# Seven instead of eight tiles transposed by TensorE in a 2:4 sparse projection, with one PSUM bank used in halves

## The chip, the cores and the metric

The kernel runs on one core of one Trainium2 chip. The metric is the device time of one execution in microseconds (us), less being better. A run's time is compared as the median of several executions; the profile is of one execution of its own.

## The reference

A weight matrix is pruned to a 2:4 pattern along its rows: in each group of four neighbouring rows, per column, the two entries that are largest in magnitude stay (ties with the second largest stay too). Then a batch of tokens is multiplied by it and a bias is added.

```python
B, S, D = 16, 512, 1024        # x: (B, S, D), w: (D, D), b: (D), all bfloat16
N, M = 2, 4
wg = w.reshape(G, M, D)
mag = jnp.abs(wg)
order = jnp.argsort(mag, 1)
thr = jnp.take_along_axis(mag, order[:, M - N:M - N + 1, :], 1)
wp = (wg * (mag >= thr)).reshape(D, D)
return jnp.einsum("bsd,df->bsf", x, wp) + b
```

## The kernel before

The 8192 tokens are 64 tiles of 128. One tile needs 16 matmuls of 128 x 128 weights against 512 columns: eight pieces of the contraction, two halves of the output columns (h = 0 and 1). TensorE needs each tile of x transposed, as its stationary operand. This is done in two ways, and the tiles are split accordingly.

**The front: the first T = 8 tiles.** While the weights are still being loaded and pruned, TensorE transposes the first eight tiles itself, in two halves g of the contraction (512 rows of the weights each). `transpose_half(g, t, bk)` (line 148) issues four transposes of 128 x 128 into the PSUM bank `bk` (line 152) and a copy on ScalarE that takes the result to the tile `xT` (line 154). In the front the contraction is split by the row within the group of four (m = 0 to 3), so that VectorE can compare the four rows without moving them between partitions.

The weights are pruned in `pieces` (line 51), each a half g and a range of columns: 0 to 128, 128 to 256 and 256 to 512 of g = 0, then 0 to 256 and 256 to 512 of g = 1 (these five are output half 0), then 512 to 1024 of g = 0 and of g = 1. `abs_piece` (line 109) takes the magnitudes, on VectorE or, for the pieces in `ABS_ON_ACT`, on ScalarE; `prep_piece` (line 120) is seven instructions on VectorE that end with the pruned piece of `wp`. `mm_piece(i, t)` (line 157) multiplies tile t by piece i: four matmuls (line 161) into the columns of bank t that belong to the piece.

There are eight PSUM banks. Tile t accumulates in bank t. The transposes of g = 0 of tile t go through bank t, ahead of its accumulation. Those of g = 1 go in turn through banks 6 and 7, and so tiles 6 and 7 begin to accumulate only after the last of these have been copied out.

The order of the front is written out by hand in the string `FRONT` (line 208), token by token; each engine gets its instructions in this order. `W` is a warm-up matmul on zeros into bank 7, `A` and `P` are the magnitudes and the pruning of a piece, `Tgt` a transpose of half g of tile t, `Mit` piece i times tile t, `Vt` the copy of output half 0 of tile t from its bank to a staging tile on ScalarE (line 176), `St` the bias added to that on VectorE (line 180), `Ugh` four DMAs that move pruned weights to the natural order of rows, tile `wp_nat` (line 144), and `Bn` the issue of the transposed load of the n-th batch of tiles (line 197). After the string a loop multiplies each of the tiles by the last piece, adds the bias (`evac_dve`, line 184) and stores the tile (line 188).

**The rest: natural tiles.** The other tiles are loaded transposed by DMA, in `batches` (line 202): tiles 8 to 11, then six batches of eight, then the last four. They use `wp_nat` and accumulate all eight pieces of the contraction in banks that are taken in turn by `next_bank`. Batch 0 does all its tiles for h = 0 and then for h = 1 (line 249); the others do both halves of a tile together (line 287). The last tile is done in four quarters.

SyncE's queue issues most loads of x and weights (lines 69 and 76), the bias, the transposed loads and the unpacks, in this order; ScalarE's queue issues a part of the first loads and the stores. There are ten output tiles `o_sb`.

Of the kernel before, what the change touches and what calls it, by code (L numbers as in the profile page):

```python
# [10 lines left out]
def kernel(  # L11
# [8 lines left out]
    P = 128  # L20
    bf16 = mybir.dt.bfloat16
# [6 lines left out]
    B, S, D = x.shape  # L28
    Dout = w.shape[1]
    KT = D // P  # L30
    NTOK = B * S
    NT = NTOK // P
    FH = 512
    KH = D // 2
    assert D == 1024 and Dout == 1024 and NT >= 24
    xf = x.flatten_outer_dims()
    of = out.flatten_outer_dims()

    T = 8

    const = ctx.enter_context(tc.tile_pool(name="const", bufs=1))
    tmp = ctx.enter_context(tc.tile_pool(name="tmp", bufs=2))
# [4 lines left out]
    bank = [psum.tile([P, FH], fp32, name=f"bank{i}") for i in range(8)]  # L47
# [1 line left out]

    wv = w.rearrange("(g p m) f -> p g m f", g=2, m=4)  # L50
    pieces = [(0, 0, 128), (0, 128, 256), (0, 256, 512), (1, 0, 256), (1, 256, 512),
              (0, 512, 1024), (1, 512, 1024)]
    loads = {"A": (0, 0, 256), "B": (0, 256, 512), "C": (1, 0, 512), "D": (0, 512, 1024), "E": (1, 512, 1024)}
    w_ld = {k: const.tile([P, 4, c1 - c0], bf16, name=f"w_{k}") for k, (g, c0, c1) in loads.items()}
    wp_gh = {(g, h): const.tile([P, 4, FH], bf16, name=f"wp_{g}_{h}") for g in range(2) for h in range(2)}
# [7 lines left out]
    def wp_of(i):  # L63
        g, c0, c1 = pieces[i]
        return wp_gh[(g, c0 // FH)][:, :, c0 % FH:c0 % FH + c1 - c0]

    def load_w(k, eng=nc.sync, m0=0, m1=4):
        g, c0, c1 = loads[k]
        K(eng.dma_start(w_ld[k][:, m0:m1, :], wv[:, g, m0:m1, c0:c1]))  # L69
# [3 lines left out]
    def load_x(g, ta, tb, eng=nc.sync):  # L73
        xt = const.tile([P, tb - ta, KH], bf16, name=f"xh_{g}_{ta}")
        src = xf[ta * P:tb * P, g * KH:(g + 1) * KH].rearrange("(t p) c -> p t c", p=P)
        K(eng.dma_start(xt[:], src))
        for t in range(ta, tb):
            xh[(g, t)] = xt[:, t - ta, :]
# [4 lines left out]
    load_x(0, 2, 4, nc.scalar)  # L83
    load_w("B")
    load_x(0, 4, 6, nc.scalar)
    load_x(0, 6, 8)
    load_x(1, 0, 2)
    load_w("C")
    load_x(1, 2, 4)
    load_x(1, 4, 8)  # L90
    load_w("D")
    load_w("E")
    bias_sb = const.tile([P, Dout], bf16, name="bias_sb")
# [9 lines left out]
    def warm(n):  # L103
        for _ in range(n):
            K(nc.tensor.matmul(bank[7][:], lhsT=zeros[:, :P], rhs=zeros[:], start=True, stop=True))  # L105
# [3 lines left out]
    def abs_piece(i, on_act):  # L109
        g, c0, c1 = pieces[i]  # L110
        n = c1 - c0
        mag = const.tile([P, 4, n], bf16, name=f"mag_{i}")[:]
        if on_act:
            K(nc.scalar.activation(mag, w_of(i), Act.Abs))
        else:
            K(nc.vector.tensor_single_scalar(
                mag.bitcast(u16), w_of(i).bitcast(u16), 0x7FFF, op=Alu.bitwise_and))
        mags[i] = mag

    def prep_piece(i):  # L120
        g, c0, c1 = pieces[i]
        n = c1 - c0
        mag = mags.pop(i)
        magv = mag.rearrange("p (a j) f -> p a j f", j=2)
        hi = tmp.tile([P, 2, FH], bf16, name="hi")[:, :, :n]
        lo = tmp.tile([P, 2, FH], bf16, name="lo")[:, :, :n]
        K(nc.vector.tensor_tensor(hi, magv[:, :, 0, :], magv[:, :, 1, :], op=Alu.max))  # L127
        K(nc.vector.tensor_tensor(lo, magv[:, :, 0, :], magv[:, :, 1, :], op=Alu.min))  # L128
        t1 = tmp.tile([P, FH], bf16, name="t1")[:, :n]
        t2 = tmp.tile([P, FH], bf16, name="t2")[:, :n]  # L130
        K(nc.vector.tensor_tensor(t1, hi[:, 0, :], hi[:, 1, :], op=Alu.min))  # L131
        K(nc.vector.tensor_tensor(t2, lo[:, 0, :], lo[:, 1, :], op=Alu.max))
        thr = tmp.tile([P, FH], bf16, name="thr")[:, :n]
        K(nc.vector.tensor_tensor(thr, t1, t2, op=Alu.max))  # L134
        mask = tmp.tile([P, 4, FH], bf16, name="mask")[:, :, :n]
        K(nc.vector.tensor_tensor(mask, mag, thr[:, None, :].to_broadcast([P, 4, n]), op=Alu.is_ge))  # L136
        K(nc.vector.tensor_tensor(wp_of(i), w_of(i), mask, op=Alu.mult))
# [4 lines left out]
    def unpack(g, h):  # L142
        for j in range(4):
            K(nc.sync.dma_start(wp_nat[h][:, 4 * g + j, :], wp_gh[(g, h)][32 * j:32 * (j + 1), :, :]))

    xT = {}

    def transpose_half(g, t, bk):
        xv = xh[(g, t)].rearrange("p (q m) -> p m q", m=4)
        dst = bank[bk][:].bitcast(bf16)[:, :4 * P].rearrange("p (m q) -> p m q", m=4)  # L150
        for m in range(4):
            K(nc.tensor.transpose(dst[:, m, :], xv[:, m, :], ident[:]))  # L152
        xt = const.tile([P, 4, P], bf16, name=f"xT_{g}_{t}")
        K(nc.scalar.copy(xt[:], dst))  # L154
        xT[(g, t)] = xt

    def mm_piece(i, t, start=False, stop=False):
        g, c0, c1 = pieces[i]
        o = c0 % FH
        for m in range(4):  # L160
            K(nc.tensor.matmul(  # L161
                bank[t][:, o:o + c1 - c0], lhsT=xT[(g, t)][:, m, :], rhs=wp_of(i)[:, m, :],
                start=start and m == 0, stop=stop and m == 3))
# [10 lines left out]
    def evac_act(t):  # L174
        st = const.tile([P, FH], fp32, name=f"stage{t}")
        K(nc.scalar.copy(st[:], bank[t][:]))  # L176
        stage[t] = st

    def add_staged(t, h):
        K(nc.vector.tensor_tensor(  # L180
            get_o(t)[:, h * FH:(h + 1) * FH], stage.pop(t)[:], bias_sb[:, h * FH:(h + 1) * FH], op=Alu.add))

    def evac_dve(t, h, bk):
        K(nc.vector.tensor_tensor(  # L184
            get_o(t)[:, h * FH:(h + 1) * FH], bank[bk][:], bias_sb[:, h * FH:(h + 1) * FH], op=Alu.add))

    def store(t):
        K(nc.scalar.dma_start(of[t * P:(t + 1) * P, :], out_tiles.pop(t)[:]))
# [3 lines left out]
    def issue_batch(t0, nb):  # L192
        if nb < 8:
            xt = const.tile([P, KT, nb * P], bf16, name=f"xTs{t0}")
        else:
            xt = xtb.tile([P, KT, nb * P], bf16, name="xTb")
        K(nc.sync.dma_start_transpose(out=xt[:], in_=xf[t0 * P:(t0 + nb) * P, :]))
        for j in range(nb):
            xN[t0 + j] = xt[:, :, j * P:(j + 1) * P]


    batches = [(8, 4)] + [(t, 8) for t in range(12, NT - 4, 8)] + [(NT - 4, 4)]

    FRONT = """
        W W W W W W W A0 A1 T00 T01 W T02 T03 P0 M00 M01 T04 T05 M02 M03 T06 T07 P1 M04 M10 M11 M05 M12 A2 T10
        M13 T11 M14 M15 T12 P2 T13 A3 M20 T14 T15 M21 M22 T16 A5 M23 T17 P3 M24 M25 A4 M30 M31 M06 M32 A6 M07  # L210
        M16 M17 M26 P4 M27 M33 M34 M35 M36 M37 M40 V0 M41 V1 M42 V2 M43 V3 M44 V4 M45 V5 M46 V6 M47 V7
        P5 B0 U00 U10 U01 M50 M51 M52 M53 M54 M55 M56 M57 P6 U11 B1 B2
        S0 S1 S2 S3 S4 S5 S6 S7
    """
    ABS_ON_ACT = (1, 5, 6)
    for tok in FRONT.split():
        k, n = tok[0], [int(c) for c in tok[1:]]
        if k == "W":
            warm(1)
        elif k == "A":  # L220
            abs_piece(n[0], n[0] in ABS_ON_ACT)
        elif k == "P":
            prep_piece(n[0])
        elif k == "T":
            g, t = n
            transpose_half(g, t, t if g == 0 else 6 + t % 2)
        elif k == "M":
            i, t = n
            mm_piece(i, t, start=i in (0, 5), stop=i in (4, 6))
        elif k == "V":  # L230
            evac_act(n[0])
        elif k == "S":
            add_staged(n[0], 0)
        elif k == "U":
            unpack(*n)
        elif k == "B":
            issue_batch(*batches[n[0]])

    for t in range(T):
        mm_piece(6, t, stop=True)  # L240
        evac_dve(t, 1, t)
        store(t)


    nbk = [0]

    def mm_nat(t, h, bk, c0=0, c1=FH):
        for kt in range(KT):
# [3 lines left out]
    def next_bank():  # L252
        bk = nbk[0] % 8
        nbk[0] += 1
        return bk
# [12 lines left out]
    for bi, (t0, nb) in enumerate(batches):  # L268
        if bi >= 1 and bi + 2 < len(batches):
            issue_batch(*batches[bi + 2])  # L270
        if bi == 0:
            for h in range(2):
                for t in range(t0, t0 + nb):
                    bk = next_bank()
# [5 lines left out]
        for t in range(t0, t0 + nb):  # L280
# [4 lines left out]
            for kt in range(KT):  # L285
                for h in range(2):
                    K(nc.tensor.matmul(bank[bks[h]][:], lhsT=xN[t][:, kt, :], rhs=wp_nat[h][:, kt, :],  # L287
                                       start=kt == 0, stop=kt == KT - 1))
# [33 lines left out]
```

## Time and profile before

| | |
|---|---|
| median of 3 runs | 237.2 us (237.07 to 237.66) |
| profiled execution | 236.98 us, of which the span of the instructions is 235.2 |
| TensorE matmuls busy | 228.7 us, 97% of the span |
| TensorE weight loads busy | 113.4 us, 48% |
| VectorE busy | 106.3 us, 45% |
| ScalarE busy | 18.1 us, 8% |
| line 287, natural tiles | 800 matmuls recorded, 175.6 us busy |
| line 161, front matmuls | 222 recorded, 29.3 us busy |
| line 249, batch 0 and the last tile | 95 recorded, 17.6 us busy |
| line 152, transposes | 64, 5.8 us busy |
| line 154, copies of transposed tiles | 16, 8.5 us busy, 591 ns each |
| HBM read and written | 4.46 MB and 16.78 MB, 90 GB/s over the span |

Engines are PE (TensorE), PEld (its weight loads, which overlap with its matmuls), DVE (VectorE), ACT (ScalarE), POOL and SP (SyncE); a q behind the name is the engine's instruction queue, here where it issues DMAs. Matmuls are pipelined: one lasts longer than the distance to the next one's start, so that distance is what it costs in a stream. Times inside the span count from its start. Some matmul records are missing in the trace.

### The profile page before, as it was taken

Reading aid. Unit: us, or ns where it says so; the run is one execution under the profiler, and the core shown is the slowest. Engines: PE = TensorE matmul, PEld = TensorE weight load, DVE = VectorE, ACT = ScalarE, POOL = GpSimd, SP = SyncE. Lnnn points to the kernel's source line nnn. Section 1 sums busy time; section 2 is a strip of 40 time slices with the busy share of each in tenths; the row PEclk is TensorE's granted clock in tenths of the full one; section 3 lists DMA queues with packets and bytes.
Section 4 is the critical chain, followed back from the end, with each engine's and each line's share of the span. In section 5 each row is a group of like instructions: output and inputs, shape, how many; then the busy total and the mean of one; then the engine's idle time right before and its main releaser. Section 6 shows DMA issues by size and latency. Waiting matters only on the chain.

```text
span 235.2 us, 2901 instructions
## 1 busy us (share of the span) xinstructions
PE 228.7 (97%) x1189; PEld 113.4 (48%) x1208; DVE 106.3 (45%) x184; ACT 18.1 (8%) x29; POOL 0.7 (0%) x6
## 2 busy tenths in 40 slices
PE   7999999999999999999999999999999999999994
PEld 3889544444444444444444444444444444444453
DVE  4999986342432442343343244234334424423433
ACT  4885400000000000000000000000000000000000
POOL 1000000000000000000000000000000000000000
PEclk9999999999999999999999999999999999999999
DMA  6999799999622299215972289421999221122122
GB/s 203 331 256 242 172 232 273 289 199 222 224 89 92 69 259 251 76 61 147 233 201 92 89 175 251 153 85 56 225 282 245 96 89 63 70 89 91 46 89 89
DMA packets 74524, 38.19 MB, mean 162 GB/s; under 512 B 59152, under 2 KB 66320, under 8 KB 74512
## 3 DMA queue, kind: packets, MB, share of 16 engines
q1 hardware_dynamic: 64624, 20.84, 42.9%
q10 hardware_dynamic: 9888, 17.17, 21.0%
q8 instruction: 9, 0.15, 0.2%
q14 instruction: 3, 0.02, 0.0%
HBM read 4.46 MB, written 16.78 MB: 90 GB/s over the span
## 4 chain that ended last, share of the span: by engine, by line
PE 93%; DMA 4%; issue 1%; ACT 0%; SPq 0%; DVE 0%
PE bank L287 75%; PE bank L161 11%; PE bank L249 7%; DMA xh<-in_x_dram 3%; DMA w_A<-in_w_dram 1%; PE bank L152 1%; ACT xT L154 0%; SPq L69 0%; DVE o_sb L265 0%
## 5 line engine op out<-in xcount | busy, mean ns | idle before, releaser
L287 PE MATMUL bank<-wp_nat,xTb 128*128 128x512 bf16 x753 | 165.1, 379 | 0.8
L184 DVE TENSOR_TENSOR o_sb<-bank,bias_sb 128x512 bf16<-128x512 f32 x118 | 76.7, 686 | 120.9 <-PE bank L287 108.7
L287 PEld LDWEIGHTS <-xTb 128*128 128x128 bf16 x768 | 75.1, 98 | 90.6
L161 PE MATMUL bank<-wp,xT 128*128 128x256 bf16 (+2 forms) x222 | 29.3, 287 | 0.1
L161 PEld LDWEIGHTS <-xT 128*128 128x128 bf16 x224 | 19.3, 98 | 8.4
L249 PE MATMUL bank<-wp_nat,xTs 128*128 128x512 bf16 (+1 forms) x95 | 17.6, 343 | 0.1
L249 PEld LDWEIGHTS <-xTs 128*128 128x128 bf16 x96 | 9.4, 98 | 8.2
L287 PE MATMUL bank<-wp_nat,xTs 128*128 128x512 bf16 x47 | 10.5, 379 | 0.1
L154 ACT COPY xT<-bank 128x512 bf16<-128x512 bf16 x16 | 8.5, 591 | 3.0 <-PE bank L152 2.9
L287 PEld LDWEIGHTS <-xTs 128*128 128x128 bf16 x48 | 4.7, 98 | 5.7
L152 PE MATMUL bank<-ident,xh 128*128 128x128 bf16 x64 | 5.8, 232 | 1.3 <-DMA xh<-in_x_dram 0.9
L152 PEld LDWEIGHTS <-xh 128*128 128x128 bf16 x64 | 4.5, 119 | 3.2 <-DMA xh<-in_x_dram 2.8
L136 DVE TENSOR_TENSOR mask<-mag,thr 128x1024 bf16<-128x1024 bf16 (+2 forms) x7 | 5.4, 769 | 0.2
L180 DVE TENSOR_TENSOR o_sb<-stage,bias_sb 128x512 bf16<-128x512 f32 x8 | 4.9, 682 | 0.0
L105 PE MATMUL bank<-zeros 128*128 128x512 bf16 x8 | 3.7, 613 | 1.2 <-DVE zeros L97 1.2
L176 ACT COPY stage<-bank 128x512 f32<-128x512 f32 x8 | 4.0, 623 | 2.6 <-PE bank L161 2.6
L127 DVE TENSOR_TENSOR hi<-mag 128x512 bf16<-128x512 bf16 (+2 forms) x7 | 3.2, 460 | 0.1
L128 DVE TENSOR_TENSOR lo<-mag 128x512 bf16<-128x512 bf16 (+2 forms) x7 | 3.2, 455 | 0.0
L134 DVE TENSOR_TENSOR thr<-t,t 128x256 bf16<-128x256 bf16 (+2 forms) x7 | 2.2, 311 | 0.2
L105 PEld LDWEIGHTS <-zeros 128*128 128x128 bf16 x8 | 1.0, 140 | 2.6 <-issue 1.4
L265 DVE TENSOR_TENSOR o_sb<-bank,bias_sb 128x256 bf16<-128x256 f32 x4 | 1.7, 422 | 1.2 <-PE bank L249 1.2
L131 DVE TENSOR_TENSOR t<-hi 128x256 bf16<-128x256 bf16 (+2 forms) x7 | 2.1, 303 | 0.0
(21 smaller groups left out, 16.2 us busy)
## 6 DMA issues: line engine op xcount, KB each, us to landing
out_dram<-o_sb ACTq DMA_DIRECT2D x63, 256.0 KB, 2.1
wp_nat<-wp SPq DMA_DIRECT2D x16, 128.0 KB, 2.8
xh<-in_x_dram SPq DMA_DIRECT2D x4, 256.0 KB, 5.7
xh<-in_x_dram ACTq DMA_DIRECT2D x2, 256.0 KB, 4.8
w_C<-in_w_dram SPq DMA_DIRECT2D x1, 512.0 KB, 6.9
xh<-in_x_dram SPq DMA_DIRECT2D x1, 512.0 KB, 7.2
w_D<-in_w_dram SPq DMA_DIRECT2D x1, 512.0 KB, 8.3
w_E<-in_w_dram SPq DMA_DIRECT2D x1, 512.0 KB, 9.9
```

Source lines behind the costliest of these rows:

```text
L105: K(nc.tensor.matmul(bank[7][:], lhsT=zeros[:, :P], rhs=zeros[:], start=True, stop=True))
L127: K(nc.vector.tensor_tensor(hi, magv[:, :, 0, :], magv[:, :, 1, :], op=Alu.max))
L128: K(nc.vector.tensor_tensor(lo, magv[:, :, 0, :], magv[:, :, 1, :], op=Alu.min))
L136: K(nc.vector.tensor_tensor(mask, mag, thr[:, None, :].to_broadcast([P, 4, n]), op=Alu.is_ge))
L152: K(nc.tensor.transpose(dst[:, m, :], xv[:, m, :], ident[:]))
L154: K(nc.scalar.copy(xt[:], dst))
L161: K(nc.tensor.matmul(bank[t][:, o:o + c1 - c0], lhsT=xT[(g, t)][:, m, :], rhs=wp_of(i)[:, m, :], start=start and m == 0, stop=stop and m = ...
L176: K(nc.scalar.copy(st[:], bank[t][:]))
L180: K(nc.vector.tensor_tensor(get_o(t)[:, h * FH:(h + 1) * FH], stage.pop(t)[:], bias_sb[:, h * FH:(h + 1) * FH], op=Alu.add))
L184: K(nc.vector.tensor_tensor(get_o(t)[:, h * FH:(h + 1) * FH], bank[bk][:], bias_sb[:, h * FH:(h + 1) * FH], op=Alu.add))
L249: K(nc.tensor.matmul(bank[bk][:, :c1 - c0], lhsT=xN[t][:, kt, :], rhs=wp_nat[h][:, kt, c0:c1], start=kt == 0, stop=kt == KT - 1))
L287: K(nc.tensor.matmul(bank[bks[h]][:], lhsT=xN[t][:, kt, :], rhs=wp_nat[h][:, kt, :], start=kt == 0, stop=kt == KT - 1))
```

## The change

Seven tiles are transposed by TensorE, T = 7, and tile 7 joins batch 0 of the natural tiles, which has five tiles then; natural tiles take bank 7 first. Bank 7 has no accumulating tile any more. The second-half transposes go through it alone, into its first 1024 bytes per partition for even tiles and its second 1024 bytes for odd ones. Output half 1 is pruned and multiplied in four pieces of 256 columns instead of two of 512, the magnitudes of all four on ScalarE. The hand-written order is new: all eight warm-up matmuls come first, T04 and T05 stand ahead of M01, the two transposes T10 and T11 follow each other, as do T12 and T13, and the magnitudes of the last pieces follow the last transpose.

```diff
-    T = 8
+    T = 7
...
     pieces = [(0, 0, 128), (0, 128, 256), (0, 256, 512), (1, 0, 256), (1, 256, 512),
-              (0, 512, 1024), (1, 512, 1024)]
+              (0, 512, 768), (0, 768, 1024), (1, 512, 768), (1, 768, 1024)]
...
-    load_x(0, 6, 8)
+    load_x(0, 6, 7)
...
-    load_x(1, 4, 8)
+    load_x(1, 4, 7)
...
-    def transpose_half(g, t, bk):
+    def transpose_half(g, t, bk, slot):
         xv = xh[(g, t)].rearrange("p (q m) -> p m q", m=4)
-        dst = bank[bk][:].bitcast(bf16)[:, :4 * P].rearrange("p (m q) -> p m q", m=4)
+        dst = bank[bk][:].bitcast(bf16)[:, slot * 4 * P:(slot + 1) * 4 * P].rearrange("p (m q) -> p m q", m=4)
...
-    batches = [(8, 4)] + [(t, 8) for t in range(12, NT - 4, 8)] + [(NT - 4, 4)]
+    batches = [(T, 12 - T)] + [(t, 8) for t in range(12, NT - 4, 8)] + [(NT - 4, 4)]
...
     FRONT = """
-        W W W W W W W A0 A1 T00 T01 W T02 T03 P0 M00 M01 T04 T05 M02 M03 T06 T07 P1 M04 M10 M11 M05 M12 A2 T10
-        M13 T11 M14 M15 T12 P2 T13 A3 M20 T14 T15 M21 M22 T16 A5 M23 T17 P3 M24 M25 A4 M30 M31 M06 M32 A6 M07
-        M16 M17 M26 P4 M27 M33 M34 M35 M36 M37 M40 V0 M41 V1 M42 V2 M43 V3 M44 V4 M45 V5 M46 V6 M47 V7
-        P5 B0 U00 U10 U01 M50 M51 M52 M53 M54 M55 M56 M57 P6 U11 B1 B2
-        S0 S1 S2 S3 S4 S5 S6 S7
+        W W W W W W W W A0 A1 T00 T01 T02 T03 P0 M00 T04 T05 M01 M02 M03 P1 A2 T06 M10 M04 M11 T10 T11 M05 M06
+        M12 M13 M14 M15 M16 P2 A3 M20 M21 T12 T13 M22 T14 M23 T15 M24 P3 T16 A5 A4 M25 M26 M30 A6 M31 M32 A7
+        M33 M34 P4 A8 M35 M36 M40 M41 V0 M42 V1 M43 V2 P5 B0 U00 U10 M44 V3 M45 V4 M46 V5 M50 V6 M51 M52 M53 P6
+        U01 M54 M55 M56 M60 M61 M62 P7 M63 M64 M65 M66 M70 M71 M72 P8 U11 B1 B2 M73 M74 M75 M76
+        S0 S1 S2 S3 S4 S5 S6
     """
-    ABS_ON_ACT = (1, 5, 6)
+    ABS_ON_ACT = (1, 5, 6, 7, 8)
...
-            transpose_half(g, t, t if g == 0 else 6 + t % 2)
+            transpose_half(g, t, t if g == 0 else 7, 0 if g == 0 else t % 2)
...
-            mm_piece(i, t, start=i in (0, 5), stop=i in (4, 6))
+            mm_piece(i, t, start=i in (0, 5), stop=i in (4, 8))
...
     for t in range(T):
-        mm_piece(6, t, stop=True)
+        mm_piece(8, t, stop=True)
...
-    nbk = [0]
+    nbk = [T]
```

More of the change, by code (lines that the diff above doesn't have):

```diff
@@ L34 @@
     KH = D // 2
-    assert D == 1024 and Dout == 1024 and NT >= 24
+    assert D == 1024 and Dout == 1024 and NT >= 24 and NT % 8 == 0
     xf = x.flatten_outer_dims()
     of = out.flatten_outer_dims()
-    T = 8
+    T = 7
     const = ctx.enter_context(tc.tile_pool(name="const", bufs=1))
```

## The prediction

> **What bounds the kernel now.** I read the engines first, then the timeline of the opening, then the table by stage and single DMA issues. Columns of a timeline row: start in us, length in us, engine, line, instruction, count, and in brackets the idle time before it with what ended it.
>
> ```profile
> PE 228.7 (97%) x1189; PEld 113.4 (48%) x1208; DVE 106.3 (45%) x184; ACT 18.1 (8%) x29; POOL 0.7 (0%) x6
> ```
>
> TensorE is the bound; nothing else is above half. So the time is what TensorE does plus what it waits.
>
> ```profile
> 4.86:15.11 10.25, 9.43 (x129) 8.37 (x130) 9.77 (x29) 7.80 (x15) 0.00 (x0) 1.00 1.05 336
> 15.11:38.60 23.49, 23.39 (x161) 14.97 (x162) 21.62 (x36) 8.24 (x12) 0.00 (x0) 1.00 1.02 211
> 38.60:52.42 13.82, 13.77 (x65) 6.25 (x64) 5.57 (x9) 0.00 (x0) 0.00 (x0) 1.00 1.21 259
> ```
>
> In the table by stage (stretch, length, then busy time and count of PE, PEld, DVE, ACT, POOL, clock, DMA) the only real idle time of PE lies before 15.11. From 38.60, the first matmul of line 249, everything streams: 64 matmuls of 512 columns in 13.82 us, 0.2158 us each. Whatever the change does is settled between the first transpose at 4.86 and that first natural matmul.
>
> ```profile
> 8.14 0.64 PE L152 MATMUL bank<-ident,xh 128*128 128x128 bf16 x8
> ...
> 9.73 0.39 PE L152 MATMUL bank<-ident,xh 128*128 128x128 bf16 x4
> ...
> 9.95 0.39 PE L161 MATMUL bank<-wp,xT 128*128 128x128 bf16 x4
> ...
> 10.15 1.07 ACT L154 COPY xT<-bank 128x512 bf16<-128x512 bf16 x2 [0.49 <-PE bank L152]
> 10.17 0.39 PE L152 MATMUL bank<-ident,xh 128*128 128x128 bf16 x4
> ...
> 11.36 0.64 PE L152 MATMUL bank<-ident,xh 128*128 128x128 bf16 x8 [0.35 <-DMA xh<-in_x_dram]
> ...
> 12.88 0.64 PE L152 MATMUL bank<-ident,xh 128*128 128x128 bf16 x8 [0.45 <-ACT xT L154]
> ...
> 13.36 1.04 PE L161 MATMUL bank<-wp,xT 128*128 128x256 bf16 x8
> ...
> 14.23 0.39 PE L152 MATMUL bank<-ident,xh 128*128 128x128 bf16 x4
> ...
> 14.45 0.60 PE L161 MATMUL bank<-wp,xT 128*128 128x256 bf16 x4
> 14.65 0.59 ACT L154 COPY xT<-bank 128x512 bf16<-128x512 bf16 x1 [0.24 <-PE bank L152]
> ```
>
> A matmul's cost is the distance to the next start. Transpose or 128 columns: 9.73 to 9.95 is four, 0.056 us each. 256 columns: 13.36 to 14.23 is eight, 0.109 us each. A token T or a 128-column M is thus 0.224, a 256-column M 0.437, a 512-column M 0.863. T10 goes into bank 6 and T11 (10.17) into bank 7 while ScalarE copies bank 6 out (10.15): two banks, no wait. The waits before 15.11 are those at 11.36 (T12, 0.52, its x) and 12.88 (T14, 0.61, its x), plus 0.11 and 0.19 before T04 (7.03) and T06 (8.14).
>
> One handover matters below. Transposes start at 14.23, their copy at 14.65: 0.42 later (0.45 when PE had been waiting, 12.88 to 13.33). The copy lasts 0.59. And from a copy's end to a waiting matmul:
>
> ```profile
> 16.95 0.58 ACT L154 COPY xT<-bank 128x512 bf16<-128x512 bf16 x1
> ...
> 17.57 0.33 PE L161 MATMUL bank<-wp,xT 128*128 128x128 bf16 x3
> ```
>
> M07 needs this copy, T17's, out of bank 7. It ends at 17.53; 0.05 later PE starts. So from the start of transposes to the start of something that needs their bank back: 0.42 + 0.59 + 0.05 = 1.06 us (1.09 after a wait).
>
> **The change, part by part.** *Tile 7 leaves the front.* T07 and T17, eight transposes, go: -0.45. Its 28 front matmuls cost 8 x 0.056 + 12 x 0.109 + 8 x 0.216 = 3.48; as a natural tile it costs 16 x 0.2158 = 3.45: -0.03. *Last pieces of 256:* 56 matmuls of 512 become 112 of 256: 56 x (0.2184 - 0.2158) = +0.15. *The eighth W:* it leaves its place between T01 and T02 for the idle 0.50 us ahead of 4.86, where its 0.43 fits; M00 can start at 6.25 instead of 6.47: -0.22.
>
> *Bank 7 in halves.* In the changed program as built, the first transposes of T11, T12, ... T16 each wait for a count of ScalarE that the copy of the tile **directly before** raises: T11 for the copy of T10, not T12 for the copy of T10. The halves differ in address only; the wait is on the bank. So two slots work as one, and each of these transposes waits out the 1.06 us less what stands between. T10/T11 and T12/T13 are adjacent in the list: 1.06 - 0.22 = 0.84 each. Ahead of T14, T15 and T16 one 256-column M stands: 1.09 - 0.25 - 0.44 = 0.40 each. Together 2.88 us. No row of before shows PE writing a bank while another engine reads it. The Trainium skill (PSUM — Partial Sum Buffer, section on bank collisions) says that two engines must not touch the same bank in the same partitions at once, whatever the address, and advises to guard by bank. By that rule halves of a bank can't serve as two buffers, and the 2.88 stands; by addresses alone it would be nothing.
>
> *Order of the front.* T04 T05 now stand ahead of M01. Their x lands no sooner:
>
> ```profile
> L76 ACTq DMA_DIRECT2D xh<-in_x_dram x1: 493/493/493, 1.8 to 1.8; - x1
> ...
> DMA to landing us min/median/max: 5.2/5.2/5.2
> ```
>
> Issued at 1.8, landed at 7.0, and T04 can't start before 7.03, as now. M00 ends at 6.47, so PE idles 0.56, which eats the W's gain and more. The other x loads lose 128 KB twice; 512 KB took 1.5 us here (landings behind the waits at 11.36 and 12.88), so the x of T06 and T10 lands 0.37 earlier and that of T14 0.75 earlier: none of them is waited for any more.
>
> The walk: T04 at 7.03; T05, M01, M02, M03 to 8.15; T06, M10, M04, M11 to 9.04; T10 at 9.04, T11 at 10.10; M05 M06 and M12 to M16 to 11.92; M20 (its piece, P2, is done at 11.08) and M21 to 12.80; T12, then T13 at 13.86; M22; T14 at 14.95; M23; T15 at 16.04; M24; T16 at 17.13, ending 17.38. From there 44 M's of 256 columns are left (M25, M26 and seven each of pieces 3 to 8): 44 x 0.437 = 19.23, to **36.61**. Five natural tiles take 5 x 16 x 0.2158 = 17.27, to 53.88, where batch 1 now starts at 52.42: **+1.46 us**. The same by terms: -0.45 - 0.03 + 0.15 - 0.22, waits gone 0.11 + 0.19 + 0.52 + 0.61 + 0.06 = -1.49, waits new 0.56 + 2.88 = +3.44, restarts after waits +0.06: +1.46. From batch 1 on nothing differs.
>
> **What must stay hidden.** *VectorE.* A 256-column piece with its abs on ScalarE takes 2.94 (14.77 to the end of its product at 17.71). ScalarE starts the abs of piece 5 only after T16's copy, at 18.1 instead of 15.13, ready near 19.15 (1.05, between 0.62 for 512 elements and 1.91 for 2048); VectorE idles 1.4 us there. P5 to P8 end at 22.1, 25.0, 28.0, 30.9; M50, M60, M70, M80 ask at 24.4, 27.4, 30.5, 33.5. Cover 2.3 us or more each. Then S0 to S6 (0.60 each) end at 35.2 and the seven evacuations at 39.4, late by 2.8; the natural tiles take bank 7 first and bank 0 at 38.3, evacuated at 35.9. *SyncE's queue.* The transposed load of four tiles was issued in 8.97 and landed in 11.0; eight took 15.5. Five land by 26 at worst, needed at 36.6; its issue takes 8.97 x 5/4, to 21.5, and the eight unpacks of half 0 behind it 0.7 each (sixteen went from 19.36 to 30.63), to 27.1. U11 waits for P8 (30.9), so B1 goes at 33.7 instead of 30.67 and lands at 49.2, needed at 53.9; B2 moves as much and has far more room. *Output tiles:* 12 for 10 buffers as before; tiles 10 and 11 wait for the first two stores, which ends one VectorE wait near 46, when that bank is not needed before 57.
>
> The profiled execution took 236.98, so it would take 238.4; the runs' median is 237.2, 0.22 above it: **238.7 us**.
>
> **Rivals.** *The halves do overlap* (the change does what it says): T12 then waits for T10's copy only. The 2.88 goes, 0.18 before T14 and 0.06 before M20 (P2) come: front ends at 33.87, -1.27, so 235.9: faster. Against it: the waits stand in the program. It decides only if T11 starts while T10's copy runs. 0.05. *The stalls stay but are cheaper:* T04's x lands half a microsecond earlier, or copies hand over faster; -0.6 to -0.9 leaves 237.7, inside 0.3% (0.7 us, about what a measurement here tells from no change). 0.09. *VectorE becomes the bound:* if half-size pieces cost as much as whole ones (4.85, from 17.63 to 22.48), P8 ends at 38.6 and the front at 41.7: +6.5, 243.7. It decides from 3.6 us a piece; the 2.94 of pieces 3 and 4 speaks against it. 0.03. *The transposed loads come late:* batch 1 waits if B1 lands after 53.9, that is 20.2 us after its issue; the longest of before took 17.8. Say one us late: 239.7. 0.03.
>
> **How the numbers follow.** The forecast has 0.80. Its own unknowns: T04's wait 0 to 0.6, each of five handovers within 0.1, the runs' scatter of 0.6 around the median: 238.0 to 239.4. Faster 0.05, same 0.10, slower 0.85.
>
> **What would show it.** Five waits of PE's line 152 for ScalarE's line 154, two near 0.84 and three near 0.40; no wait for x after 7.03; the first natural matmul at 36.6 and batch 1 at 53.9. Copies of one half running beside transposes of the other would prove it wrong, as would PE waiting for a piece or for the transposed x.

## The result and the profile after

| | before | changed |
|---|---|---|
| median | 237.07 us (237.01 to 237.66, 5 runs) | 238.82 us (238.30 to 239.75, 5 runs) |
| ratio, 95% interval | | 1.007 (1.0044 to 1.0096) |
| profiled execution, its span | 236.98, 235.2 | 238.60, 236.8 |
| first natural matmul (line 249) | 38.60 | 36.78 |
| first matmul of batch 1 (line 287) | 52.42 | 54.05 |

The change makes the kernel 1.75 us slower. The profiled executions differ by 1.62 us and batch 1 starts 1.63 us later, so the whole difference has arisen by then. The front is 1.82 us shorter, but one natural tile more costs 3.45.

The table by stage of the changed kernel (stretch, length, then busy time and count of PE, PEld, DVE, ACT, POOL, clock, DMA share, GB/s):

```profile
4.68:17.56 12.88, 10.14 (x133) 9.11 (x133) 12.26 (x35) 7.22 (x13) 0.00 (x0) 1.00 1.09 299
17.56:36.78 19.22, 19.22 (x181) 17.22 (x178) 17.31 (x40) 7.89 (x12) 0.00 (x0) 1.00 0.77 176
36.78:54.05 17.27, 17.16 (x81) 7.84 (x81) 8.50 (x14) 0.00 (x0) 0.00 (x0) 1.00 1.21 251
54.05:234.20 180.15, 178.93 (x833) 82.85 (x847) 67.92 (x107) 0.00 (x0) 0.00 (x0) 1.00 0.52 142
```

From 17.56 on PE waits for nothing (busy shares under 100% there come from matmul records that the trace lacks). Before that it idles 2.74 us out of 12.88. What it waits for stands in the list of waits (engine and line, what was waited for: us in all, times, longest):

```profile
PE bank L152 <- ACT xT L154: 2.1, 5, 0.7
PEld L152 <- DMA xh<-in_x_dram: 1.7, 2, 0.9
...
PE bank L152 <- DMA xh<-in_x_dram: 0.7, 1, 0.7
```

Five times a transpose waits for a copy of the line 154; the list for before has one such entry of 0.4, at 12.88, where the weight load names T14's x instead, which landed then. The timeline of the changed kernel shows each of the five, from T04 to the last transpose:

```profile
7.36 0.64 PE L152 MATMUL bank<-ident,xh 128*128 128x128 bf16 x8 [0.68 <-DMA xh<-in_x_dram]
...
9.40 0.39 PE L152 MATMUL bank<-ident,xh 128*128 128x128 bf16 x4
...
9.82 0.59 ACT L154 COPY xT<-bank 128x512 bf16<-128x512 bf16 x1 [0.31 <-PE bank L152]
10.46 0.38 PE L152 MATMUL bank<-ident,xh 128*128 128x128 bf16 x4 [0.68 <-ACT xT L154]
...
13.11 0.39 PE L152 MATMUL bank<-ident,xh 128*128 128x128 bf16 x4
13.54 0.58 ACT L154 COPY xT<-bank 128x512 bf16<-128x512 bf16 x1 [2.08 <-PE bank L152]
...
14.17 0.38 PE L152 MATMUL bank<-ident,xh 128*128 128x128 bf16 x4 [0.67 <-ACT xT L154]
...
15.23 0.38 PE L152 MATMUL bank<-ident,xh 128*128 128x128 bf16 x4 [0.24 <-ACT xT L154]
...
16.29 0.38 PE L152 MATMUL bank<-ident,xh 128*128 128x128 bf16 x4 [0.24 <-ACT xT L154]
...
17.34 0.38 PE L152 MATMUL bank<-ident,xh 128*128 128x128 bf16 x4 [0.24 <-ACT xT L154]
```

T10 goes at 9.40, its copy at 9.82, and T11, into the other half of the bank, at 10.46, right behind the copy. The same from T12 (13.11) to T13 (14.17) to T14 (15.23), and on to T15 (16.29) and T16 (17.34): always 1.05 to 1.06 us from transposes to transposes, whichever half they use. The idle time in brackets is counted from the modelled end of the matmul before, which lies 0.16 behind the point at which PE could have issued the next (9.40 + 0.39 against 9.40 + 4 x 0.056). With it, 0.68 and 0.24 become the 0.84 that an adjacent pair loses and the 0.40 of the others. Two and three of them are 2.88 us.

T04 waits at 7.36 for its x. That load was issued at 1.8 in both profiles and landed 5.2 us later before, 5.5 here:

```profile
L76 ACTq DMA_DIRECT2D xh<-in_x_dram x1: 491/491/491, 1.8 to 1.8; - x1
...
DMA to landing us min/median/max: 5.5/5.5/5.5
```

### The profile page after: what moved, and what is told of

Read it like the earlier page. It is cut to its first block, busy times and chain, and to the rows that moved or that the text cites. A ratio compares the mean times of both kernels' runs of the same rounds, so it can differ in the third digit from the quotient of the medians.

```text
span 236.8 us, 2986 instructions
## 1 busy us (share of the span) xinstructions
PE 228.9 (97%) x1226; PEld 118.1 (50%) x1244; DVE 107.3 (45%) x198; ACT 17.1 (7%) x28; POOL 0.7 (0%) x6
## 4 chain that ended last, share of the span: by engine, by line
PE 94%; DMA 2%; ACT 1%; issue 1%; ACTq 0%; DVE 0%
PE bank L287 74%; PE bank L161 10%; PE bank L249 9%; DMA xh<-in_x_dram 2%; PE bank L152 1%; ACT xT L154 1%; ACTq L76 0%; ACTq L69 0%; DVE o_sb L265 0%
## 5 line engine op out<-in xcount | busy, mean ns | idle before, releaser
L161 PE MATMUL bank<-wp,xT 128*128 128x256 bf16 (+1 forms) x252 | 25.8, 261 | 0.0
L161 PEld LDWEIGHTS <-xT 128*128 128x128 bf16 x252 | 22.2, 98 | 2.1
L249 PE MATMUL bank<-wp_nat,xTs 128*128 128x512 bf16 (+1 forms) x110 | 21.0, 348 | 0.1
L249 PEld LDWEIGHTS <-xTs 128*128 128x128 bf16 x112 | 11.0, 98 | 9.8
L287 PEld LDWEIGHTS <-xTs 128*128 128x128 bf16 x48 | 4.7, 97 | 5.7
L136 DVE TENSOR_TENSOR mask<-mag,thr 128x1024 bf16<-128x1024 bf16 (+1 forms) x9 | 5.7, 633 | 0.3
L127 DVE TENSOR_TENSOR hi<-mag 128x512 bf16<-128x512 bf16 (+1 forms) x9 | 3.5, 392 | 1.6 <-ACT mag L114 1.5
L128 DVE TENSOR_TENSOR lo<-mag 128x512 bf16<-128x512 bf16 (+1 forms) x9 | 3.5, 389 | 0.0
L134 DVE TENSOR_TENSOR thr<-t,t 128x256 bf16<-128x256 bf16 (+1 forms) x9 | 2.5, 277 | 0.3
L131 DVE TENSOR_TENSOR t<-hi 128x256 bf16<-128x256 bf16 (+1 forms) x9 | 2.4, 269 | 0.0
L132 DVE TENSOR_TENSOR t<-lo 128x256 bf16<-128x256 bf16 (+1 forms) x9 | 2.4, 269 | 0.0
```

The lines of the kernel that those rows point to most:

```text
L161: K(nc.tensor.matmul(bank[t][:, o:o + c1 - c0], lhsT=xT[(g, t)][:, m, :], rhs=wp_of(i)[:, m, :], start=start and m == 0, stop=stop and m = ...
L249: K(nc.tensor.matmul(bank[bk][:, :c1 - c0], lhsT=xN[t][:, kt, :], rhs=wp_nat[h][:, kt, c0:c1], start=kt == 0, stop=kt == KT - 1))
```

## Experiments

Two figures are read from each profile: the start of the first natural matmul, which is the front's end, and its distance from the start of T04. The second leaves out how late T04's x happened to land, and everything else that stands ahead of T04; between the two nothing in the changed kernel waits for a load. In the changed kernel it is 36.78 - 7.36 = 29.42 us; the table takes it from unrounded times. The kernel before ran beside each group (medians 237.07 to 237.15, and 236.96 beside the last two runs).

| run | median us (range) | ratio to before, 95% interval | T04 | front's end | distance |
|---|---|---|---|---|---|
| change | 238.82 (238.30 to 239.75) | 1.0070 (1.0044 to 1.0096) | 7.36 | 36.78 | 29.42 |
| one half only | 238.38 (238.29 to 238.66) | 1.0054 (1.0040 to 1.0067) | 7.20 | 36.61 | 29.41 |
| spread out | 235.97 (235.57 to 236.28) | 0.9951 (0.9937 to 0.9965) | 7.21 | 33.77 | 26.56 |
| two banks | 236.28 (236.15 to 236.36) | 0.9962 (0.9950 to 0.9975) | 6.80 | 34.34 | 27.53 |
| pieces of 512 | 238.75 (238.68 to 239.34) | 1.0073 (1.0061 to 1.0086) | 6.99 | 36.92 | 29.93 |
| one pair back | 236.53 (236.17 to 237.54) | 0.9971 (0.9956 to 0.9986) | 7.11 | 34.67 | 27.56 |
| W back | 239.24 (238.98 to 240.13) | 1.0097 (1.0073 to 1.0121) | 7.74 | 37.16 | 29.42 |
| M01 first | 238.26 (238.19 to 238.52) | 1.0045 (1.0029 to 1.0062) | 7.29 | 36.46 | 29.17 |
| filled | 235.66 (235.41 to 236.11) | 0.9935 (0.9921 to 0.9950) | 7.43 | 33.58 | 26.15 |
| change again | 238.59 (238.27 to 240.34) | 1.0077 (1.0052 to 1.0102) | 7.58 | 37.00 | 29.42 |
| W back again | 238.67 (238.06 to 240.25) | 1.0075 (1.0049 to 1.0102) | 7.89 | 37.30 | 29.42 |

### Only one half of the bank

```diff
-            transpose_half(g, t, t if g == 0 else 7, 0 if g == 0 else t % 2)
+            transpose_half(g, t, t if g == 0 else 7, 0)
```

> All second-half transposes of the changed kernel go into the first half of bank 7; the order and all else stay. Theory (the wait is on the bank, so the second half adds nothing): the first matmul of line 249 stays at 36.8 us, the five waits for the copies stay at 0.84, 0.84, 0.40, 0.40, 0.40, and the time at 238.8 us within 0.3%. Rival (the second half lets at least some transposes run beside a copy, and the change is slower for another reason): taking it away costs up to five waits more, and the time is 0.5 to 2.5 us above 238.8.

The second half was worth nothing: the distance is the same to 0.01 us, and the time is not above the change's. PE's timeline in this kernel has the same pattern, shifted by T04's earlier start:

```profile
9.23 0.39 PE L152 MATMUL bank<-ident,xh 128*128 128x128 bf16 x4
10.29 0.38 PE L152 MATMUL bank<-ident,xh 128*128 128x128 bf16 x4 [0.67 <-ACT xT L154]
...
12.95 0.39 PE L152 MATMUL bank<-ident,xh 128*128 128x128 bf16 x4
14.01 0.39 PE L152 MATMUL bank<-ident,xh 128*128 128x128 bf16 x4 [0.67 <-ACT xT L154]
```

The waits in the two built programs are the same, so this could hardly have come out otherwise. What it shows is that halves and one buffer are the same kernel in time.

### Two banks in place of two halves

```diff
-            transpose_half(g, t, t if g == 0 else 7, 0 if g == 0 else t % 2)
+            transpose_half(g, t, t if g == 0 else 7 - t % 2, 0)
...
-        ... T10 T11 M05 M06
-        M12 M13 M14 M15 M16 P2 A3 M20 M21 T12 T13 M22 T14 M23 T15 M24 P3 T16 A5 A4 M25 M26 M30 A6 ...
+        ... T10 T11 M05
+        M12 M13 M14 M15 P2 A3 M20 M21 T12 T13 M22 T14 M23 T15 M24 P3 T16 A5 A4 M25 M06 M16 M26 M30 A6 ...
```

> The changed kernel in its own order, T10 T11 and T12 T13 still adjacent, but odd tiles transpose their second half through bank 6 instead of the second half of bank 7; tile 6's first three M move behind T16 for that. Theory (bank, not order, makes the wait): the 0.84 waits of T11 and T13 vanish, T14 keeps about 0.2, M20 waits 0.3 for its piece; the first matmul of line 249 at 34.4 us and the time 236.4 us. Rival (the handover PE to ScalarE and back costs it wherever the data lie): the waits of 0.84 stay and the time stays at 238.8.

The order is that of the change with T10 T11 and T12 T13 adjacent, and the waits inside the pairs are gone. In PE's timeline of this kernel the eight transposes of a pair are one block:

```profile
8.84 0.61 PE L152 MATMUL bank<-ident,xh 128*128 128x128 bf16 x8
9.29 1.28 PE L161 MATMUL bank<-wp,xT 128*128 128x128 bf16 x20
11.21 1.03 PE L161 MATMUL bank<-wp,xT 128*128 128x256 bf16 x8 [0.64 <-DVE wp L137]
12.08 0.61 PE L152 MATMUL bank<-ident,xh 128*128 128x128 bf16 x8
```

The copies last 0.59 as before; for the pairs only the bank differs. So it is the shared bank that makes the wait. T14, which goes into bank 7 behind T12, still starts 1.06 after it, at 13.14: M22 ahead of it ends 0.17 sooner (0.2 was expected). Each bank is a single tile of the program (`bank[7]`), so the runs don't tell whether its waits go by the bank or by that tile. PE now meets the next bound: at 11.21 it waits for piece 2, whose product VectorE ends at 11.15, hardly sooner than in the change (11.21). With the 0.16 of above this costs 0.80 instead of the 0.3 expected, since T04 came 0.56 sooner in this run and P2 didn't.

### The transposes spread out

```diff
-        W W W W W W W W A0 A1 T00 T01 T02 T03 P0 M00 T04 T05 M01 M02 M03 P1 A2 T06 M10 M04 M11 T10 T11 M05 M06
-        M12 M13 M14 M15 M16 P2 A3 M20 M21 T12 T13 M22 T14 M23 T15 M24 P3 T16 A5 A4 M25 M26 M30 A6 M31 M32 A7
-        M33 M34 P4 A8 M35 M36 M40 M41 V0 M42 ...
+        W W W W W W W W A0 A1 T00 T01 T02 T03 P0 M00 T04 T05 M01 M02 M03 P1 A2 T06 M10 M04 M11 T10 M05 M06 M12
+        M13 M14 T11 M15 M16 P2 A3 M20 M21 T12 M22 M23 M24 T13 M25 M26 P3 T14 A5 A4 M30 M31 M32 T15 A6 M33
+        M34 P4 T16 A7 A8 M35 M40 M41 V0 M36 M42 ...
```

> The changed kernel with its transposes of the second half spread out in the hand-written order, at least five 128-column or two 256-column tokens M between two of them; bank 7 in halves as it was, the magnitudes of pieces 5 to 8 earlier. Theory (the stalls of 2.88 us are what the change costs, and other work fits into them): no wait of a transpose for a copy above 0.1 us, the first matmul of line 249 at 33.9 instead of 36.8 us, and 235.9 us, below the kernel before (237.1). Rival (TensorE would wait for pruned pieces or x in the same place): waits of piece 2 or of x take up most of it, front end above 36, 238 us or more.

Bank 7 alone, in halves, is enough if other work stands between: the distance falls by 29.42 - 26.56 = 2.86 us, the five stalls of 2.88, and the kernel is faster than before. In PE's timeline of this kernel every second-half transpose follows the matmuls ahead of it with no idle time. T11 (10.59) and T12 (12.13), as an example:

```profile
9.47 1.28 PE L161 MATMUL bank<-wp,xT 128*128 128x128 bf16 x20
10.59 0.39 PE L152 MATMUL bank<-ident,xh 128*128 128x128 bf16 x4
10.81 1.48 PE L161 MATMUL bank<-wp,xT 128*128 128x128 bf16 x16
12.13 0.39 PE L152 MATMUL bank<-ident,xh 128*128 128x128 bf16 x4
```

### One pair put back

```diff
-        M13 M14 T11 M15 M16 P2 A3 M20 M21 T12 M22 M23 M24 T13 M25 M26 P3 T14 A5 A4 ...
+        M13 M14 T11 M15 M16 P2 A3 M20 M21 T12 T13 M22 M23 M24 M25 M26 P3 T14 A5 A4 ...
```

(against the spread order)

> The spaced order of the run before (235.97 us, first matmul of line 249 at 33.77), with T12 and T13 adjacent again and nothing else between the two sides changed: one stall out of five put back. Theory (each stall is 0.42 + 0.59 + 0.05 us from transposes to transposes, less what stands between, and is paid in full): one wait of T13 for a copy of 0.84, front end later by 0.84, 34.6, and 236.8 us. Rival (TensorE has slack later in the front, and a single stall is swallowed by it): front end within 0.3 of 33.8 and 236.0 us.

The front ends 0.90 us later, at 34.67, the time rises by 0.56, from 235.97 to 236.53. The distance grows by 1.00: 0.84 is the one wait (T12 at 12.20, T13 at 13.26 in PE's timeline), and 0.17 a wait for piece 2 ahead of M20, since T04 came 0.10 sooner than in the spread run. A single stall is paid in full at the front's end; nothing later in the front takes it in. The medians, of two groups, show less than the profiles, 0.56 against 0.90, with runs that spread over 1.4 us, and the two ratios' intervals overlap: the price is shown by the timeline, and the times don't contradict it.

### Pieces of 512 again

```diff
-              (0, 512, 768), (0, 768, 1024), (1, 512, 768), (1, 768, 1024)]
+              (0, 512, 1024), (1, 512, 1024)]
...
-    ABS_ON_ACT = (1, 5, 6, 7, 8)
+    ABS_ON_ACT = (1, 5, 6)
```

(and the tokens of pieces 7 and 8 taken out)

> The changed kernel with the last weight pieces 512 columns wide as before (two instead of four), all else as in the change. Theory: TensorE saves 0.15 us of matmuls, but piece 5 is ready only at about 25.3 (its magnitudes start at 18.25 behind the last copy and take 1.9, VectorE 4.9 more) while its first matmul could go at 24.7, so it waits 0.6: first matmul of line 249 at 37.2, 239.3 us. Rival (narrow pieces are a cost of their own): 0.15 to 0.5 us faster than 238.8.

The front behaves as expected: the distance grows by 0.51. The timeline shows M50 held until piece 5 is done:

```profile
23.54 1.22 DVE L137 TENSOR_TENSOR wp<-w_D,mask 128x2048 bf16<-128x2048 bf16 x1
24.82 0.55 PEld L161 LDWEIGHTS <-xT 128*128 128x128 bf16 x4 [0.75 <-DVE wp L137]
24.82 0.82 PE L161 MATMUL bank<-wp,xT 128*128 128x512 bf16 x3 [0.48 <-ACT stage L176]
```

The product ends at 24.76 and the weight load of M50 starts 0.06 later; ScalarE, which the matmul's own row names, had copied bank 0 out by 22.35. The wait is 0.64 (0.48 and the 0.16 of above), less 0.15 for fewer matmuls. The medians don't show it, 238.75 against the change's 238.59 and 238.82. In the profiles T04's x landed 0.36 sooner here than in the change's first, and the front ends 0.14 later all the same. So the narrow pieces cost no more than their 0.15, and they hide the late start of ScalarE's magnitudes.

### The eighth warm-up matmul, and M01

```diff
-        W W W W W W W W A0 A1 T00 T01 T02 T03 P0 ...
+        W W W W W W W A0 A1 T00 T01 W T02 T03 P0 ...
```

> The changed kernel with the eighth warm-up matmul put back between T01 and T02. Theory (its earlier place gains nothing in the end, since T04 waits for its x): M00 starts 0.1 to 0.3 later, T04 starts when its x has landed all the same (7.0 to 7.4), first matmul of line 249 at 36.6 to 36.9 and 238.6 us. Rival (its place is worth 0.2 to 0.4): the front ends above 37.0 and the time is 239.0 us.

The first run was 0.42 us above the change's first median, as the rival had it, but in its profile x landed at 7.69, 0.38 later than in the change's. So both were run again beside each other.

> The changed kernel once more, beside the next run on the same chip, for the place of the eighth warm-up matmul. Both theories: 238.3 to 238.9 us; the x of T04 lands somewhere from 6.8 to 7.7, and from T04's start to the first matmul of line 249 it is 29.42 us as in its first profile.

> The changed kernel with the eighth warm-up matmul between T01 and T02, once more. Theory (its place gains nothing, and the 239.24 us of the run before came from a late landing of x): within 0.3% of the changed kernel beside it, both fronts 29.42 us from T04's start to line 249. Rival (its place is worth 0.4 us): slower by 0.3 to 0.6 us than the kernel beside it, again with a later T04.

Side by side they differ by 0.08 us (238.59 and 238.67). In all four profiles T04 waits for its x and the distance behind it is 29.42, so what M00 gains ahead of T04 is lost in that wait. The place of this matmul is worth nothing that can be measured here.

```diff
-        ... P0 M00 T04 T05 M01 M02 M03 P1 ...
+        ... P0 M00 M01 T04 T05 M02 M03 P1 ...
```

> The changed kernel with M01 ahead of T04 and T05 again. Theory (PE idles 0.6 to 0.9 us before T04, and M01's 0.22 fits into that): from T04's start to the first matmul of line 249 it is 29.20 instead of 29.42 us, and the time is 0.2 us less, 238.4. Rival (M01's operand, copied by ScalarE, comes too late): no difference in that distance.

The distance falls by 0.25 us, to 29.17, but M01 (0.22) now stands ahead of the stretch, so it would fall by about that in any case. Whether M01 fits into the wait for x is not shown: in this profile x had landed at 7.10 and T04 started at 7.29, right behind M01, so that there was no wait left to fill (the last section says why). The time is 0.3 to 0.6 below the change's two medians, of which the landing of x may hold a part.

### What is left in the front

```diff
-        ... T00 T01 T02 T03 P0 M00 T04 T05 M01 M02 M03 P1 A2 T06 M10 M04 M11 T10 M05 M06 M12
-        M13 M14 T11 M15 M16 P2 A3 M20 M21 T12 M22 M23 M24 T13 M25 M26 P3 T14 A5 A4 M30 M31 M32 T15 A6 M33
-        M34 P4 T16 A7 A8 M35 M40 M41 V0 M36 M42 ...
+        ... T00 T01 T02 T03 P0 M00 M01 M02 T04 T05 M03 P1 A2 T06 M10 M04 T10 M11 M05 M12 M06
+        T11 M13 M14 M15 M16 T12 P2 A3 M20 M21 M22 T13 M23 M24 T14 A5 M25 M26 P3 A4 T15 A6 M30 M31 M32 T16 A7 A8 M33
+        M34 P4 M35 M36 M40 M41 V0 M42 ...
```

(against the spread order)

> The spaced order, with M01 and M02 in the idle time before T04 and T12 ahead of M20. Theory (what is left to gain in the front is the wait for x before T04, and behind it VectorE, which ends piece 2 only at 11.2): front end 33.55 to 33.7 instead of 33.77, 235.8 us, hardly below the spaced order. Rival (the 0.45 us of M01 and M02 are gained in full): front end 33.3, 235.5 us.

This is the lowest median, 235.66 us, 0.65% below the kernel before (0.50 to 0.79%), though its interval overlaps that of the spread order. The front ends at 33.58, as expected, and not at the rival's 33.3. Here too M01 and M02 stand ahead of T04 and have left the distance. Its front, from T00 to the first natural matmul, has PE busy throughout:

```profile
4.79:33.58 28.79, 28.79 (x308) 26.61 (x309) 27.80 (x70) 14.62 (x25) 0.00 (x0) 1.00 0.97 239
```

VectorE is busy for 27.80 of the same 28.79 us. This suggests that little more is to be had by the order of tokens alone; no order beyond this one was tried.

## Why the prediction was right

**The forecast** was 238.7 us, by 1.46 us more than before; it became 238.82, by 1.75 more in the medians and 1.62 in the profiled executions.

- *Bank 7 in halves, 2.88 us.* Measured 0.84, 0.84, 0.40, 0.40 and 0.40. The handover of 0.42 + 0.59 + 0.05, taken from T16 and M07 of the old profile, is 1.05 to 1.06 in every turn of the new one. The bound of 1.09 for a start after a wait wasn't reached: a transpose that had waited for a copy rather than a load handed over as fast as others. Spread out, the same transposes in the same bank gave the 2.86 back; in two banks, with the pairs still adjacent, the pairs' waits of 0.84 were gone.
- *The rule of the Trainium skill (PSUM — Partial Sum Buffer, section on bank collisions),* that a bank and not an address is what two engines must not share, is how the program was built: the wait is one that the program sets. No run shows what the chip would do without it; a kernel whose waits go by address wasn't tried.
- *Tile 7's leaving, the 256-column matmuls and the moved W* (-0.45, -0.03, +0.15, -0.22). From 17.56 PE's 44 tokens took 19.22 us, worked out as 19.23, and the five natural tiles 17.27, as worked out. The moved W gave M00 a start of 6.29, worked out as 6.25, and it was swallowed by T04's wait as written.
- *T04's wait, 0.56.* This term was mis-sized: PE sat from 6.52 to 7.36, 0.84 us, outside the 0 to 0.6 that I had allowed, since x landed at 7.31 instead of 6.98. T04 so came 0.33 later than worked out; the three handovers without the 0.03 after a wait gave 0.1 of it back, small differences 0.06 more, and the front ended 0.17 later. That the median lies within 0.2 us of the forecast is partly luck: the landing of x alone moved the profiled executions of this kernel from 238.60 to 238.82.
- *The cover on VectorE and SyncE* held. P5 to P8 ended at 22.3, 25.1, 28.0 and 30.8 (22.1, 25.0, 28.0, 30.9 worked out), and PE waited for none. The last evacuation of the seven tiles ended at 39.2 (39.4 worked out) and held up nothing. Batch 1 started without a wait.
- *The rivals.* Overlapping halves: refuted by the pairs in the profile. VectorE as the bound: not in the changed kernel; with pieces of 512 PE waits 0.64 us for it, with two banks 0.80 and with one pair back 0.17 for piece 2. Cheaper stalls through an earlier x: x landed anywhere from 6.8 to 7.8 in these profiles and moved the time with it, but no run of the change (238.27 at the least) came down to one of the kernel before (237.88 at the most).

## What to carry to other kernels

Two halves of a PSUM bank were not two buffers in this program: where TensorE fills one while another engine drains the other, the program's wait is on the bank, and the pair runs one after the other. Before giving a bank away or halving one, work out the handover from the old profile (fill to copy, copy, copy to the next fill) and see whether the order holds that much other work between two uses; here five 128-column or two 256-column tokens M were enough, and no stall was left. Two versions that differ by the landing of one early load are best compared from the instruction that waits for it; what is moved ahead of that instruction, as M01 was, has then to be judged by the time.

## What was not expected of the hardware

The same load, issued at 1.78 to 1.79 in every profile, landed anywhere between 6.76 and 7.84 us, and in the kernels that wait for it the run's time followed: in the four profiles of the change and of W back it landed at 7.31, 7.54, 7.69 and 7.84, and these executions took 238.60, 238.82, 238.98 and 239.13 us, the same steps to 0.02. The wider spread of the change's runs (238.27 to 240.34) is not explained by it in full: the run of 240.34 had a span of 237.4, so that most of its excess lies outside the span. What makes the load land late was not looked into.

TensorE's transposes started out at 107 ns each, from start to start, and went over to 56 at different points of the same stretch. Rows of the sixteen first transposes in the change's two profiles (start, length), the first profile and then the second; in the first the starts are 107 ns apart up to 6.2, in the second only up to 4.9:

```profile
4.68 1.77 PE L152 MATMUL bank<-ident,xh 128*128 128x128 bf16 x16
```

```profile
4.76 1.12 PE L152 MATMUL bank<-ident,xh 128*128 128x128 bf16 x16
```

Nothing came of it in these two, because T04 waited for x in both. The Trainium skill (TensorE: Matmul & The Clock Gate, Part 1) says that the clock is raised at the end of a window that runs free of the kernel, so that the point wanders by half a microsecond either way; here the rows change over at 6.2 and at 4.9, 1.3 us apart, somewhat more than that. In three other profiles it was late enough to matter, 6.9 (one half only), 7.1 (filled) and 7.2 (M01 first): there T04 started at 7.20, 7.43 and 7.29 although its x had landed at 7.03, 6.84 and 7.10.
